# A gated MLP on linear attention: 1088 output columns cut into 364, 362 and 362 instead of 424, 332 and 332, with other starting addresses and a new order

## The chip, the cores and the metric

The kernel runs on one core of a Trainium2 chip. The metric is the device time of one execution in microseconds (us). A core has a matrix engine (TensorE, PE), three engines for element-wise work (VectorE or DVE, ScalarE or ACT, GpSimd or POOL), and SyncE (SP), which issues the DMAs here. Each engine runs its own instructions in the order in which they were written; engines wait for each other by semaphores.

## What is computed

```python
def _attn_ref(q, k, v, S1, S2):                     # 4 batches, 4 heads, 1088 positions, d = 32
    def phi(x):                                     # 8 x 8 = 64 features
        a = np.einsum('rd,bhsd->bhsr', S1, x)
        b = np.einsum('rd,bhsd->bhsr', S2, x)
        return np.einsum('bhsi,bhsj->bhsij', a, b).reshape(*x.shape[:-1], r * r)
    q_p, k_p = (phi(q), phi(k))
    kv = np.einsum('bhsf,bhsd->bhfd', k_p, v)
    z = np.sum(k_p, axis=2)
    num = np.einsum('bhsf,bhfd->bhsd', q_p, kv)
    den = np.einsum('bhsf,bhf->bhs', q_p, z)[..., None] + 1e-06
    return num / den

def _moe_ref(x, w_in, w_spatial, b_spatial, w_out): # x: 4 x 1088 x 128
    h = np.maximum(x @ w_in, 0.0)                   # 1024 wide
    u, v = (h[..., :512], h[..., 512:])
    v_n = (v - mean(v)) / np.sqrt(var(v) + 1e-06)
    v_s = np.einsum('ts,bsd->btd', w_spatial, v_n) + b_spatial[None, :, None]
    return (u * v_s) @ w_out                        # w_out: 512 x 128
```

## The kernel before

**Precision.** Every large product is made of two-part operands: a value is rounded to a "high" part and its remainder is the "low" part. `mm3` (L424) is then three matmuls: high by high (L425), high by low (L426), low by high (L427). `split` (L502) makes the parts: ACT casts the high one (L504), DVE subtracts to get the low one (L435), on POOL in some cases (L438).

**Tiling.** The 1088 output positions (the columns of a matmul's streamed operand) are cut into three chunks `CH`; the 512 gated features into four blocks d of 128; the 1088 input positions into nine row blocks kt (eight of 128 and one of 64). For each batch b, block d and chunk c (48 in all) `main` (L829) issues
- `hidden`: three matmuls of one `mm3` into the PSUM bank `pu` and a relu on ACT into a tile u (L935),
- `spatial`: 26 matmuls into a bank `sp`: nine L943 (vh by the high weights), eight L945 (vl by the high weights), eight L952 (vh by the low weights) and one L954 for the last row block, which has the bias in two extra rows,
- `gate`: DVE multiplies sp by u (L979) and the product is split into gh and gl,
- `out_mm`: three matmuls of one `mm3` into the bank `po`, which sums over d; after the last d, ACT or DVE copies it out (L917, L919) and SP stores it (L922).

v is the stationary operand (tiles vh, vl), the spatial weights are streamed (tile wT, high and low halves, with the bias rows in its last row block). Batch 0 goes through chunk 0 for all four d at once, first a high pass over kt (its four accumulators are in two sp and two po banks), then a low pass, because v's row blocks come one after another from the layer norm (L799 to L824, split by L889, L892 and L898, L901). The other (b, d, c) follow one by one. The attention of a batch runs beside the main part of the batch before it; batch 0's runs ahead (`attention0`).

**Loads.** Weights come in pieces through the staging tiles `pl` (L432), ACT casts the high part (L551), DVE or POOL subtracts the low part (L554). w_in and w_out are 64-bit floats and are decoded by integer arithmetic (L487 to L500). The bias is loaded once (b32), split, and each half is copied to a row of wT by DMAs on SP (L568), one for each piece of `BIAS`.

**Homes in memory.** Most tiles rotate through as many buffers as `SB_BUFS` says; an instruction that writes a new tile waits for the last reader of the old one in its buffer. Before, chunk 0 (424 columns) of batches 0 and 3 had homes of its own (`big`): u and the copied output in the kp tiles, and the two parts of the gate in the two buffers of the xh or xl tiles. All other gates use three u and three g buffers. Modulo 256 bytes, the stationary tiles vh, wih0, woh began at 96 and vl, wil0, wol at 224; chunk 0 of wT at 32 and chunks 1 and 2 at 240; g at 32 or 240.

**What sets the order.** All instructions are first collected by the class `Order` (L117) with their costs and readers, and are then put into one order for each engine by a list scheduler: due times come backwards from `T_MAIN`, `PACE` and the costs (`c_mm` from the table `C_MM` and so on), and the table `LEADS` moves groups or single instructions ahead or back by nanoseconds. Into gaps that the planner expects on PE in the first 50 us it puts small filling matmuls (L452).

## Time and profile before

| | us |
|---|---|
| median of 3 runs | 330.75 (330.46 to 331.38) |
| profiled execution | 331.01 |
| its span | 329.2 |
| main loop of batch 0 begins (first L943) | 31.84 |
| last matmul begins | 325.78 |

A row of the timeline is: start, duration, engine, line, operation, output<-inputs, shapes, count, and in brackets idle time of that engine just before and who ended it. Matmuls are pipelined: their durations overlap, and what one costs is the distance to the start of the next. A row of the windows view is: stretch, its length, then busy time and (count) of PE, PE's weight loads, DVE, ACT and POOL, the granted clock of PE, the share of the DMA engines and GB/s. SPq is SP's queue of DMA issues. Names are the program's, with buffer numbers left out.

### The profile page before, as it was taken

The page shows a single profiled execution, that of the slowest core. Times are in us where ns is not written, and L with a number is a line of the kernel's source. Part 1 is how long each engine was busy: PE and PEld are TensorE (multiplying, and loading weights), DVE is VectorE, ACT ScalarE, POOL GpSimd, SP SyncE. Part 2 cuts the span into 40 slices and gives each one's busy share as a digit, 9 for nine tenths or more (in the row PEclk, how much of TensorE's full clock was granted, in tenths as well). Part 3 has the DMA queues.
Part 4 walks back from the last instruction along what each step waited for, and adds up shares of the span by engine and source line. Part 5 has one row for each costly group of instructions (what it writes and reads, how often), then busy time and mean ns, then how long its engine had stood idle before and what let it go on. Part 6 is the DMA issues. An engine that isn't in the chain of part 4 may idle for free.

```text
span 329.2 us, 6032 instructions
## 1 busy us (share of the span) xinstructions
PE 323.0 (98%) x2308; PEld 311.2 (95%) x2308; DVE 200.3 (61%) x449; ACT 158.0 (48%) x365; POOL 59.4 (18%) x69
## 2 busy tenths in 40 slices
...
PEclk9999999999999999999999999999999999999999
...
GB/s 218 304 94 51 122 136 277 153 131 161 60 47 44 20 127 147 148 2 24 47 96 1 77 111 60 2 0 0 3 0 2 0 47 23 0 2 1 0 2 68
DMA packets 18365, 23.10 MB, mean 70 GB/s; under 512 B 3104, under 2 KB 18080, under 8 KB 18336
## 3 DMA queue, kind: packets, MB, share of 16 engines
...
q14 instruction: 11, 0.09, 0.1%
...
## 4 chain that ended last, share of the span: by engine, by line
PE 76%; DVE 9%; ACT 5%; DMA 5%; SPq 2%; issue 1%; DVEq 0%; ACTq 0%
PE sp L943 18%; PE sp L945 16%; PE sp L952 16%; PE sd L425 3%; PE sd L426 3%; PE sd L427 3%; PE po L426 2%; DMA pl<-in_wT 2%; PE pu L425 2%; SPq L432 2%; DVE wT L554 2%; PE pu L427 2%; PE pu L426 2%; PE po L427 2%; PE po L425 2%; PE sd L638 2%
## 5 line engine op out<-in xcount | busy, mean ns | idle before, releaser
L943 PE MATMUL sp<-wT,vh 128*128 128x332 f32 (+1 forms) x414 | 134.4, 325 | 0.0
L945 PE MATMUL sp<-wT,vl 128*128 128x332 f32 (+1 forms) x368 | 119.1, 324 | 0.0
L952 PE MATMUL sp<-wT,vh 128*128 128x332 f32 (+1 forms) x368 | 116.9, 323 | 0.0
L943 PEld LDWEIGHTS sp<-wT,vh 128*128 128x128 f32 x414 | 77.9, 188 | 1.3
L945 PEld LDWEIGHTS sp<-wT,vl 128*128 128x128 f32 x368 | 69.2, 188 | 0.6
L952 PEld LDWEIGHTS sp<-wT,vh 128*128 128x128 f32 x368 | 69.1, 188 | 0.2
L979 DVE TENSOR_TENSOR u<-sp,u 128x332 f32<-128x332 f32 (+1 forms) x40 | 20.5, 514 | 38.3 <-PE sp L954 26.9
L435 DVE TENSOR_TENSOR g<-u,g 128x332 fp32r<-128x332 f32 (+1 forms) x38 | 21.7, 570 | 25.7 <-PE po L426 18.9
L504 ACT CAST g<-u 128x332 fp32r<-128x332 f32 (+1 forms) x38 | 17.9, 485 | 40.2 <-DVE u L979 25.8
L935 ACT ACTIVATE u<-pu 128x332 f32<-128x332 f32 (+1 forms) x40 | 18.5, 463 | 36.1 <-PE pu L427 35.1
L801 DVE BATCH_NORM_STATS2 st<-vt 128x6 f32<-128x512 f32 x36 | 24.2, 688 | 5.1 <-ACT vt L799 4.9
L779 DVE RECIPROCAL c<-c 128x384 f32<-128x384 f32 (+1 forms) x9 | 21.8, 2418 | 9.2 <-ACT c L777 9.2
L799 ACT ACTIVATE vt<-sd 128x512 f32<-128x512 f32 x36 | 21.4, 601 | 10.9 <-PE sd L427 10.3
L748 POOL TENSOR_TENSOR pl<-pl,pl 128x384 f32<-128x384 f32 (+1 forms) x18 | 19.0, 1059 | 33.6 <-DMA pl<-abT 33.4
L861 ACT CAST vh<-vt 128x384 fp32r<-128x384 f32 x36 | 17.4, 510 | 14.4 <-DVE vt L821 8.4
L438 POOL TENSOR_TENSOR r<-pl,r 128x384 fp32r<-128x384 f32 (+1 forms) x18 | 17.5, 982 | 37.1 <-ACT r L504 37.0
L863 DVE TENSOR_TENSOR vl<-vt,vh 128x384 fp32r<-128x384 f32 (+1 forms) x36 | 20.2, 578 | 2.8 <-ACT vh L861 2.7
L821 DVE TENSOR_SCALAR vt<-vt,mv,sm 128x512 f32<-128x512 f32 x32 | 17.4, 579 | 0.0
L438 POOL TENSOR_TENSOR r<-c,r 128x384 fp32r<-128x384 f32 (+1 forms) x9 | 9.7, 1082 | 40.0 <-ACT r L504 40.0
L425 PE MATMUL pu<-x,wih 128*128 128x332 f32 (+1 forms) x48 | 16.0, 334 | 0.8 <-ACT kp L935 0.8
L426 PE MATMUL pu<-x,wih 128*128 128x332 f32 (+1 forms) x48 | 15.7, 327 | 0.0
L427 PE MATMUL pu<-x,wil 128*128 128x332 f32 (+1 forms) x48 | 15.7, 327 | 0.0
(161 smaller groups left out, 522.2 us busy)
## 6 DMA issues: line engine op xcount, KB each, us to landing
...
```

The lines of the kernel that those rows point to most:

```text
L425: nc.tensor.matmul(o, ah, bh, start=start, stop=False)
L426: nc.tensor.matmul(o, ah, bl, start=False, stop=False)
L427: nc.tensor.matmul(o, al, bh, start=False, stop=stop)
L435: return lambda: nc.vector.tensor_tensor(out=o(), in0=a(), in1=bb(), op=ALU.subtract)
L438: return lambda: nc.gpsimd.tensor_tensor(out=o(), in0=a(), in1=bb(), op=ALU.subtract)
L779: op("DVE", 135 + 6.3 * n, lambda x32=x32, n=n: nc.vector.reciprocal(out=x32[:, :n], in_=x32[:, :n]), w=[x32])
L799: op("ACT", c_act(512, True), lambda pv=pv, t=t: nc.scalar.activation(vt[:, t], pv.ap, AF.Relu), r=[pv], w=[(vt, t)])
L801: op("DVE", 690, lambda stats=stats, t=t: nc.vector.bn_stats(out=stats.ap, in_=vt[:, t]), r=[(vt, t)], w=[stats])
L943: nc.tensor.matmul(sp[:, :cw], vh[:, kt], wTh[:, kt, cs], start=(kt == 0), stop=False)
L945: nc.tensor.matmul(sp[:, :cw], vl[:, kt], wTh[:, kt, cs], start=False, stop=False)
L952: nc.tensor.matmul(sp[:, :cw], vh[:, kt], wTl[:, kt, cs], start=False, stop=False)
L979: op("DVE", c_dve(cw), lambda: nc.vector.tensor_tensor(out=u.ap, in0=sp[:, :cw], in1=u.ap, op=ALU.mult), r=[sp], w=[u], lead=LEAD[1])
```

## The change

- The chunks are 364, 362 and 362 columns wide and begin at 0, 384 and 768 of a row block's 1152.
- wT, the g and the r buffers lie in one tile `moving` that is shifted by four elements, so that each of them begins at 176 modulo 256 bytes. The six stationary tiles follow each other, and all begin at 160. x now begins at 0 (32 before) and the second half of w_in, which is streamed too, at 64 (160 before).
- `big` is gone: every gate of every batch uses the three u and the three g buffers (r in the last block, as before), and the output copies use u (vt in the last batch).
- `pl` has seven buffers instead of six.
- The bias is cut into five pieces instead of three (364, 360 and 2, 360 and 2 columns), so ten instead of six DMAs copy it to wT.
- `C_MM` has the new sizes, and nearly all of `LEADS`'s 1,600 numbers are new. The order is new on every engine; fewer filling matmuls are put in.

```diff
-CH = [(0, 424), (424, 332), (756, 332)]
-AT = [0, 436, 820]
-PITCH, G_PITCH, G_AT = 1152, 448, {424: 0, 332: 52}
-BIAS = [(0, 8, 53), (8, 4, 83), (12, 4, 83)]
+CH = [(0, 364), (364, 362), (726, 362)]
+AHEAD, LINE = 4, 64
+AT = [0, 384, 768]
+PITCH = 1152
+BIAS = [(0, 4, 91), (4, 4, 90), (8, 2, 1), (10, 4, 90), (14, 2, 1)]
+BIAS_AT = [(0, 0), (1, 0), (1, 360), (2, 0), (2, 360)]
...
-    "pl": 6, "c": 3, "r": 4, "abT": 2, "kt": 3, "v": 3, "ka": 2, "kp": 3, "kvh": 1, "kvl": 1,
+    "pl": 7, "c": 3, "r": 4, "abT": 2, "kt": 3, "v": 3, "ka": 2, "kp": 3, "kvh": 1, "kvl": 1,
...
-LEADS = {'W0': 13650, 'W0.0': -12650, 'W0.2': -20000, 'W0.3': -8660, 'W0.4': -12950,
+LEADS = {'W0': 12110, 'W0.0': 1680, 'W0.1': 19860, 'W0.3': 18270, 'W0.4': -770, 'W0.5': -8890,
...
-C_MM = {424: 188.5, 332: 148.5}
+C_MM = {364: 162.0, 362: 161.0}
 def c_mm(n, k=1):
...
-    homes["ka", 0] = const.tile([P, 96], F32, name="ka0")
-    fixed["b32"], fixed["mask_sb"] = const.tile([P, 16], F32, name="b32"), const.tile([P, 6], F32, name="mask_sb")
-    weights("vh", "wih0", "woh")
-    homes["ka", 1] = const.tile([P, 96], F32, name="ka1")
-    weights("vl", "wil0", "wol")
+    fixed["mask_sb"] = const.tile([P, 6], F32, name="mask_sb")
+    weights("vh", "vl", "wih0", "wil0", "woh", "wol")
+    n_w, n_g, n_r = 2 * NS * PITCH, SB_BUFS["g"] * 384, SB_BUFS["r"] * 384
+    moving = const.tile([P, 2 * AHEAD + n_w + n_g + n_r], F32R, name="moving")[:, AHEAD:]
+    homes["wT"] = moving[:, :n_w]
+    homes |= {("g", i): moving[:, n_w + 384 * i:n_w + 384 * (i + 1)] for i in range(SB_BUFS["g"])}
+    homes |= {("r", i): moving[:, n_w + n_g + 384 * i:n_w + n_g + 384 * (i + 1)] for i in range(SB_BUFS["r"])}
...
-    homes["wT"] = const.tile([P, 2 * NS * PITCH], F32R, name="wT")
-    homes["g"] = const.tile([P, SB_BUFS["g"], G_PITCH], F32R, name="g")
...
-        if t.tag == "g":
-            at = G_AT[t.shape[1]]
-            return homes["g"][:, t.slot, at:at + t.shape[1]]
...
     def load_bias():
-        b32 = tl(None, "b32", [83, 16])
+        b32 = tl(None, "b32", [91, 16])
...
-        bh, bl = tl(None, "bh", [83, 16], F32R), tl(None, "bl", [83, 16], F32R)
+        bh, bl = tl(None, "bh", [91, 16], F32R), tl(None, "bl", [91, 16], F32R)
...
-        for c, (at, w, rows) in enumerate(BIAS):
+        for (at, w, rows), (c, c0) in zip(BIAS, BIAS_AT):
...
-                cs = slice(AT[c], AT[c] + w * rows)
+                cs = slice(AT[c] + c0, AT[c] + c0 + w * rows)
...
-                    r=[t], w=[(wTl, ("bias", c, n))], kb=2,
+                    r=[t], w=[(wTl, ("bias", c, c0, n))], kb=2,
...
     def load_sq():
...
-        def big(c):
-            return c == 0 and (wide or not b)
...
         def due(cost):
...
-                ob = tl("vt" if wide else "kp" if big(c) else "u", f"ob{b}{c}", [P, cw])
+                ob = tl("vt" if wide else "u", f"ob{b}{c}", [P, cw])
...
                 def copy(eng, at, n, key):
...
-            u = tl("kp" if big(c) else "u", f"u{b}{d}{c}", [P, cw])
+            u = tl("u", f"u{b}{d}{c}", [P, cw])
...
-                r += [(wTl, (kt, c))] + ([(wTl, ("bias", c, 0)), (wTl, ("bias", c, 1)), vx] if kt == NK else [])
+                r += [(wTl, (kt, c))] + ([*((wTl, ("bias", c, c0, n)) for x, c0 in BIAS_AT if x == c for n in range(2)), vx] if kt == NK else [])
             def f():
...
         def gate(d, c, sp, u):
...
-            if big(c):
-                g = tl(("xh", "xl")[d % 2], f"g{b}{d}{c}", [P, 2, G_PITCH], F32R)
-                parts = [(lambda: g[:, 0, :cw], (g, 0)), (lambda: g[:, 1, :cw], (g, 1))]
-            else:
-                tag = "r" if last(d) else "g"
-                gh, gl = tl(tag, f"gh{b}{d}{c}", [P, cw], F32R), tl(tag, f"gl{b}{d}{c}", [P, cw], F32R)
-                parts = [(lambda: gh.ap, gh), (lambda: gl.ap, gl)]
-            (hi, wh), (lo, wl) = parts
-            split(hi, lo, lambda: u.ap, cw, [u], [wh], [wl])
-            return hi, lo, [wh, wl]
+            tag = "r" if last(d) else "g"
+            gh, gl = tl(tag, f"gh{b}{d}{c}", [P, cw], F32R), tl(tag, f"gl{b}{d}{c}", [P, cw], F32R)
+            split(lambda: gh.ap, lambda: gl.ap, lambda: u.ap, cw, [u], [gh], [gl])
+            return lambda: gh.ap, lambda: gl.ap, [gh, gl]
...
-    bias = np.zeros((83, 16), moe_b_spatial.dtype)
-    for (c0, cw), (at, w, rows) in zip(CH, BIAS):
-        bias[:rows, at:at + w] = moe_b_spatial.reshape(-1)[c0:c0 + cw].reshape(rows, w)
+    bias = np.zeros((91, 16), moe_b_spatial.dtype)
+    for (at, w, rows), (c, c0) in zip(BIAS, BIAS_AT):
+        c0 += CH[c][0]
+        bias[:rows, at:at + w] = moe_b_spatial.reshape(-1)[c0:c0 + w * rows].reshape(rows, w)
...
```

Line numbers behind the table of sizes are 2 lower in the new kernel (L425 is L423, L554 is L552), and 6 lower in `main` (L943 is L937).

**SP, from the last weight pieces ahead of the bias to w_out.** Rows are line, operation, output<-source, shape. pl is a staging tile, bh and bl are the bias's halves. Before:

```order
L432 DMA pl_229<-in_wT 128x424
L432 DMA pl_77<-in_wT 128x424
L568 DMA wT<-bh 1x53x8
L568 DMA wT<-bh 1x83x4 x2
L568 DMA wT<-bl 1x53x8
L568 DMA wT<-bl 1x83x4 x2
L432 DMA pl_196<-in_wT 128x424
L432 DMA kt<-in_w_out 128x4x256
L432 DMA pl_187<-in_wT 128x424
```

Now:

```order
L430 DMA pl_246<-in_wT 128x364
L430 DMA pl_80<-in_wT 128x364
L566 DMA moving<-bh 1x91x4
L566 DMA moving<-bh 1x2x1 x2
L566 DMA moving<-bh 1x90x4 x2
L566 DMA moving<-bl 1x91x4
L566 DMA moving<-bl 1x2x1 x2
L430 DMA pl_224<-in_wT 128x364
L566 DMA moving<-bl 1x90x4 x2
L430 DMA kt<-in_w_out 128x4x256
L430 DMA pl_222<-in_wT 128x364
```

Ten bias DMAs instead of six stand ahead of the load of w_out (kt<-in_w_out). Further ahead, the cast of bh, for which the first of them waits, stood on ACT behind three casts of weights; now it stands ahead of them.

**DVE, around the low halves of v's row blocks 6 and 7 of batch 0** (the L892 x2 of before, L886 x2 now). Rows are line, operation, output<-inputs, shape; L554 and L552 make the low part of a piece of the weights, L821 and L819 normalise a block of v. Before:

```order
L812 SCALAR_TENSOR_TENSOR sm_507<-sm_517,sm_507 128x3
L554 TENSOR_TENSOR wT<-pl_187,wT 128x424
L812 SCALAR_TENSOR_TENSOR sm_537<-mv_474,sm_507 128x3
L554 TENSOR_TENSOR wT<-pl_77,wT 128x424
L821 TENSOR_SCALAR vt_164<-vt_164,mv_474,sm_507 128x512
L554 TENSOR_TENSOR wT<-pl_196,wT 128x424
L821 TENSOR_SCALAR vt_164<-vt_164,mv_474,sm_507 128x512
L892 TENSOR_TENSOR vl<-vt_164,vh 128x512 x2
L554 TENSOR_TENSOR wT<-pl_227,wT 64x424
L901 TENSOR_TENSOR vh<-vt_164,vh 64x512
```

Now:

```order
L810 SCALAR_TENSOR_TENSOR sm_512<-sm_520,sm_512 128x3
L552 TENSOR_TENSOR moving<-pl_222,moving 64x364
L810 SCALAR_TENSOR_TENSOR sm_543<-mv_481,sm_512 128x3
L886 TENSOR_TENSOR vl<-vt_98,vh 128x512
L819 TENSOR_SCALAR vt_161<-vt_161,mv_481,sm_512 128x512 x2
L886 TENSOR_TENSOR vl<-vt_161,vh 128x512 x2
L552 TENSOR_TENSOR moving<-pl_191,moving 128x364
L488 TENSOR_SCALAR v<-v 128x512
L552 TENSOR_TENSOR moving<-pl_224,moving 128x364
L552 TENSOR_TENSOR moving<-pl_207,moving 128x362
L895 TENSOR_TENSOR vh<-vt_161,vh 64x512
```

Ahead of the two low halves stood three low parts of chunk 0's weights in these rows, and one stands there now; the others moved behind them, among decoding steps of w_out (L488).

**PE, the first output product of chunk 1 in batch 0** (po_146<-g before, po_121<-moving now, where moving is the streamed tile that also holds g). Before:

```order
L945 MATMUL sp_301<-wT,vl 128x332
L952 MATMUL sp_301<-wT,vh 128x332
L425 MATMUL po_261<-x,woh 128x424
L426 MATMUL po_261<-x,woh 128x424
L427 MATMUL po_261<-x,wol 128x424
L425 MATMUL po_146<-g,woh 128x332
L426 MATMUL po_146<-g,woh 128x332
L427 MATMUL po_146<-g,wol 128x332
L943 MATMUL sp_301<-wT,vh 128x332
L945 MATMUL sp_301<-wT,vl 128x332
```

Now:

```order
L636 MATMUL sd_123<-v,kp_144 64x66 x12
L636 MATMUL sd_123<-v,kp_157 64x66 x12
L937 MATMUL sp_262<-moving,vh 128x362
L948 MATMUL sp_262<-moving,v_83 128x362
L937 MATMUL sp_302<-moving,vh 128x362
L939 MATMUL sp_302<-moving,vl 128x362
L946 MATMUL sp_302<-moving,vh 128x362
L423 MATMUL po_121<-moving,woh 128x362
L424 MATMUL po_121<-moving,woh 128x362
L425 MATMUL po_121<-moving,wol 128x362
```

Before, this product came right behind the last output product of chunk 0, and its gate stood on DVE behind that chunk's; now it stands 87 rows further on, behind 36 small attention products (L636, twelve a row) and more of the spatial stream.

2 lines of the change are left out of this document (1 added, 1 removed).

## The prediction

> **What bounds the kernel now.** I read the page's busy shares and chain first, then busy time by stretch, then the timeline, where the starts of successive matmuls give what one of them costs (their durations overlap). The durations come from one profiled execution of 331.01 us, of which 329.2 us is the span; the median of the runs shown is 330.75, 0.26 lower.
>
> ```profile
> PE 323.0 (98%) x2308; PEld 311.2 (95%) x2308; DVE 200.3 (61%) x449; ACT 158.0 (48%) x365; POOL 59.4 (18%) x69
> PEclk9999999999999999999999999999999999999999
> 31.80:43.40 11.60, 11.60 (x60) 11.16 (x59) 11.46 (x28) 9.86 (x23) 2.33 (x2) 1.00 0.45 130
> 200.00:300.00 100.00, 100.00 (x607) 98.36 (x607) 47.11 (x103) 36.12 (x82) 5.38 (x7) 1.00 0.02 8
> ```
>
> TensorE is busy 98% of the span at the full granted clock, and in the stretch from 200 to 300 us nothing else comes near. The time is therefore the sum of matmul gaps, plus a few stalls, plus the start and the end. Only in the first 50 us is another engine as full: from 31.8 to 43.4 DVE is busy 11.46 of 11.60 us. So four things can change: the gap of a matmul, the stalls, the prologue, the tail.
>
> **Size of a matmul.** Each row block is now streamed in 364, 362 and 362 columns instead of 424, 332 and 332. The columns (1088) and the matmuls are the same. There are 16 pairs of batch and block, with 26 spatial, 3 hidden and 3 output matmuls for each chunk, so 32 x 16 = 512 triples of matmuls.
>
> ```profile
> 222.70 0.31 PE L943 MATMUL sp<-wT,vh 128*128 128x332 f32 x1
> ...
> 226.66 0.39 PE L425 MATMUL sd<-wih,x 128*128 128x512 f32 x1
> 233.33 0.35 PE L943 MATMUL sp<-wT,vh 128*128 128x424 f32 x1
> ...
> 234.09 0.35 PE L945 MATMUL sp<-wT,vl 128*128 128x424 f32 x1
> ...
> 237.08 0.32 PE L943 MATMUL sp<-wT,vh 128*128 128x332 f32 x1
> ```
>
> From 222.70 to 226.66 stand 27 matmuls of 332 columns: 146.7 ns each. From 234.09 to 237.08 stand 16 of 424: 186.9 ns. The four just before, after the change of size, took (234.09 - 233.33) / 4 = 190 ns: a stream needs a few matmuls to settle. The line through 146.7 and 186.9 gives 160.7 at 364 and 159.8 at 362, so a triple costs 480.3 before and after: **0 by this line**. Short runs of the same sizes can be read too:
>
> ```profile
> 150.35 0.31 PE L425 MATMUL pu<-x,wih 128*128 128x332 f32 x1
> ...
> 150.81 0.32 PE L425 MATMUL po<-g,woh 128*128 128x332 f32 x1
> 24.64 0.36 PE L425 MATMUL pu<-x,wih 128*128 128x424 f32 x1
> ...
> 25.22 0.39 PE L425 MATMUL sd<-wih,x 128*128 128x512 f32 x1
> 47.10 0.34 PE L425 MATMUL sd<-r,sqh 128*128 128x384 f32 x1
> ...
> 47.62 1.12 PE L952 MATMUL sp<-wT,vh 128*128 128x424 f32 x5
> ```
>
> Three of 332 take 0.46 us (153 each), three of 424 take 0.58 (193), three of 384 take 0.52 (173). The line from 153 to 193 would give 176 at 384; the measured 173 lies below it. By the line from 332 to 384 a triple would cost 165.3 + 164.5 + 164.5 = 494.3 instead of 193 + 2 x 153 = 499: 5 ns less, or 2.6 us in 512 triples. I keep both ends, 0 and -2.6, and take 2 ns a triple, nearer to the settled row because most of the stream is long runs: **-1.0 us**. No other engine is as full there, so all of it lies on the path.
>
> The Trainium skill (TensorE: Matmul & The Clock Gate, Back-to-back issue gap) gives the gap of an isolated warm matmul as columns / 2.4 plus 2.5 ns. By it a triple costs 460.8 ns under either cut, so the cut alone would change nothing; the trace's 146.7 at 332 columns is 5.9 ns above that rule's 140.8 and its 186.9 at 424 is 7.7 above 179.2, so the trace does not bear the fixed 2.5 out.
>
> The new starting addresses (176 modulo 256 bytes for what is streamed, 160 for the weights) I cost at nothing: the stream of before settles alike on weights at 96 and at 224, vh and vl alternating in the rows above. That it doesn't settle on the new ones is a rival below.
>
> **Breaks.** Counted in the two orders, the spatial stream is cut by other matmuls into 125 pieces before and 111 now, and 775 against 715 matmuls stand among the first nine of a piece. At 190 - 186.9, about 3 to 5 ns each, 60 fewer of them are **-0.25 us**.
>
> **Stalls.** Two output products waited on the split of their gate:
>
> ```profile
> 62.85 0.31 PE L425 MATMUL po<-g,woh 128*128 128x332 f32 x1
> 63.52 0.42 PE L426 MATMUL po<-g,woh 128*128 128x332 f32 x1 [0.35 <-DVE g L435]
> 63.77 0.31 PE L427 MATMUL po<-g,wol 128*128 128x332 f32 x1
> 107.06 0.31 PE L425 MATMUL po<-g,woh 128*128 128x332 f32 x1
> 107.92 0.41 PE L426 MATMUL po<-g,woh 128*128 128x332 f32 x1 [0.56 <-DVE g L435]
> 108.17 0.31 PE L427 MATMUL po<-g,wol 128*128 128x332 f32 x1
> ```
>
> Against 0.15 a matmul, the first lost 0.52 + 0.10, the second 0.71 + 0.10: 1.4 us together. The new order puts the first product of chunk 1 87 rows further down, past 36 small products, and the others also further behind their gates, so these waits go. What is late next is batch 0's supply from DVE:
>
> ```profile
> 37.72 0.59 DVE L554 TENSOR_TENSOR wT<-pl,wT 128x424 fp32r<-128x424 f32 x1
> 38.23 0.54 DVE L821 TENSOR_SCALAR vt<-vt,mv,sm 128x512 f32<-128x512 f32 x1
> ...
> 39.20 1.24 DVE L821 TENSOR_SCALAR vt<-vt,mv,sm 128x512 f32<-128x512 f32 x1
> 40.36 1.28 DVE L892 TENSOR_TENSOR vl<-vt,vh 128x512 fp32r<-128x512 f32 x2
> 39.13 1.03 POOL L438 TENSOR_TENSOR r<-c,r 128x384 fp32r<-128x384 f32 x1 [5.27 <-ACT r L504]
> ```
>
> PE now runs through chunk 0's high pass at 364/424 of its pace (about 0.167 instead of 0.195 a matmul) and asks for row block 6's low half at the 48th matmul, 31.84 + 47 x 0.167 = 39.7; before it had it at 40.96 (the pair of 40.36 ends at 41.57, 0.60 each). The new DVE order takes two weight rows from ahead of it (2 x 0.51) and shortens the two that remain (2 x 0.06): 39.8. The L821 of 39.20 took 1.24 beside POOL's L438, against 0.46 for the one of 38.23; if the two part, 39.1. So the margin is between -0.1 and 0.6, and the same at row block 8 and at the last low weight rows of chunk 0. For these, and for other products now tight behind their gates, I allow 0.8 in all. Net **-0.6 us**; bounds -1.4 and +1.2.
>
> **Prologue.** Ten bias transfers instead of six stand on SP ahead of w_out:
>
> ```profile
> 8.23 0.31 SPq L432 DMA_DIRECT2D b<-in_bsp  x1
> 15.99 2.04 SPq L568 DMA_DIRECT2D wT<-bh  x3
> 18.13 1.83 SPq L568 DMA_DIRECT2D wT<-bl  x3
> 20.06 0.53 SPq L432 DMA_DIRECT2D pl<-in_wT  x1
> 20.69 0.69 SPq L432 DMA_DIRECT2D kt<-in_w_out  x1
> 15.76 0.21 ACT L504 CAST bh<-b 83x16 fp32r<-83x16 f32 x1
> 25.20 0.67 ACT L487 ACTIVATE v<-kt 128x512 f32<-128x512 f32 x1 [0.46 <-DMA kt<-in_w_out]
> 26.45 0.52 ACT L935 ACTIVATE kp<-pu 128x424 f32<-128x424 f32 x1
> 27.02 0.46 PE L425 MATMUL pu<-x,wih 128*128 128x424 f32 x1 [0.61 <-ACT kp L935]
> 31.84 0.36 PE L943 MATMUL po<-wT,vh 128*128 128x424 f32 x1
> ```
>
> ACT waits 0.46 for w_out; behind it in ACT's row stands the L935 that empties the bank for the hidden product, for which PE waits 0.61, and from there PE runs without a gap into the main loop at 31.84. So a later w_out moves the main loop one for one. The bias cast now comes ahead of two weight casts and one of 512 columns instead of behind them, some 1.4 us earlier at about 0.45 each. Six long transfers at 2.04 / 3 to 1.83 / 3 and four of two elements at between 0.31 (the issue of b) and 0.61 make 5.1 to 6.4 instead of 3.97: w_out is issued 0 to 1.3 us later. The small matrices S1 and S2 (in_sks) are now loaded second on SP instead of first, and one filler stands ahead of PE's first projection (some 0.25); that is hidden by ACT's 0.46, and gone with it. I take **+0.6 us** (0 to 1.3).
>
> **Tail.**
>
> ```profile
> 324.13 0.50 DVE L435 TENSOR_TENSOR g<-u,g 128x332 fp32r<-128x332 f32 x1
> 325.78 0.32 PE L427 MATMUL po<-r,wol 128*128 128x332 f32 x1
> 326.13 0.44 ACT L917 COPY vt<-po 128x332 f32<-128x332 f32 x1 [0.87 <-PE po L427]
> ```
>
> Five output triples again follow the last gate. One split now reuses a g tile two triples after its last reader; its chain of 0.94 (two of 0.50, overlapping) just fits 2 x 0.48. The copies grow by 0.02. **+0.1 us**.
>
> **Sum:** -1.0 - 0.25 - 0.6 + 0.6 + 0.1 = -1.15 on 331.01 = 329.86 by the profiled execution; against the median 330.75, **329.6 us**.
>
> **Rivals.**
> 1. **No change**: the size term is 0 by the settled line and the removed stalls come back whole at other gates (0 - 0.25 + 0 + 0.6 + 0.1): 331.2; with half of the stalls gone 330.3; about 330.75. For it: every product still has its gate's split ahead of it on DVE. Against: the longer distances. The rule of the Trainium skill named above also gives 0 for the size term.
> 2. **Slower, the stream doesn't settle** at the new addresses, in all spatial runs. About half of the 1,536 matmuls, some 700, now stand at the settled 147 and 187; each would pay 3.1 (190 - 186.9) to 6.3 (153 - 146.7): 2.2 to 4.5 us. 333.0. It decides from about half of them on.
> 3. **Slower, three small homes**: chunk 0's gates of batch 0 had wide homes; now four gates share three u and three g tiles, a gate's low half waits for an earlier output product, and DVE, which runs in order, holds the weight rows behind it. Three such waits at the price of those above (0.62 to 0.81) are +2.2 us: 331.8, or 332 where w_out is late as well. It decides once DVE is over 0.3 us later than in my walk.
> 4. **Much faster**: the size term at its low end and no new waits: 329.6 - 1.6 - 0.8 = 327.2.
>
> **Chances.** Forecast (328.6 to 330.6) 0.45, rival 1 0.20, rival 2 0.09, rival 3 0.13, rival 4 0.13. The range reaches from rival 4 to past rival 3, 327.0 to 332.7, leaving out half of rival 4, most of rival 2 and the far ends. A measurement of this kernel tells about 0.3% (1.0 us) from no change. Faster than 329.76: rival 4, 0.6 of the forecast and a little of rival 1, 0.42. Slower than 331.74: rival 2, most of rival 3 and a little of rival 1, 0.23. Within: 0.35.
>
> **What would show it.** Gaps in a long run of 364 near 160 (right), 165 or more (rival 2). ACT's wait for w_out at 0.5 to 1.7 us, and the first spatial matmul at 32.4. No wait of PE on L433 at the first product of chunk 1; waits between 38 and 46 us below 0.6. PE's last matmul about 3 us before the span's end. Wrong would make it a wait that appears in batches 1 and 2, which I went through only by distances.

## The result, and the profile after

The changed kernel takes **339.27 us** (median of 4 runs, 338.85 to 340.18) against 330.62 us for the kernel before (4 runs beside it): a ratio of **1.0261, 95% interval 1.0234 to 1.0288**. It is slower, and outside of the range that was given. The profiled execution took 339.48 us, with a span of 337.7 against 329.2.

From the page of the changed kernel, the busy times and TensorE's granted clock by slices:

```profile
PE 327.2 (97%) x2304; PEld 313.9 (93%) x2304; DVE 204.7 (61%) x449; ACT 159.1 (47%) x365; POOL 61.6 (18%) x69
PEclk9999999999999999999999999999999999999999
```

Busy time by stretch (PE, PEld, DVE, ACT and POOL with their counts, then the clock), first two stretches of the kernel before, then three of the changed kernel:

```profile
31.84:60.00 28.16, 28.16 (x156) 27.56 (x155) 22.97 (x50) 19.62 (x47) 9.38 (x9) 1.00 0.66 191
90.00:130.00 40.00, 39.44 (x270) 37.05 (x270) 32.39 (x74) 23.43 (x59) 12.78 (x13) 1.00 0.36 72
```

```profile
33.69:60.00 26.31, 25.37 (x150) 24.25 (x149) 25.69 (x53) 19.19 (x44) 7.97 (x7) 1.00 0.61 180
90.00:130.00 40.00, 37.91 (x218) 35.76 (x217) 34.13 (x75) 25.38 (x60) 11.30 (x12) 1.00 0.30 64
200.00:300.00 100.00, 100.00 (x685) 97.96 (x684) 50.60 (x110) 40.08 (x92) 10.83 (x12) 1.00 0.10 22
```

In this execution the granted clock is whole throughout, so a lower clock explains nothing of it. (The other three runs have a mean granted clock of 0.993 to 0.995, and no trace says where it fell; their times, 338.85 to 340.18, lie on both sides of this one.) TensorE, idle 0.56 us between 90 and 130 before, is idle 2.09 there now. From the start of the main loop to 60 us it was never idle before, with DVE busy 22.97 of 28.16 us; now it is idle 0.94, with DVE busy 25.69 of 26.31. From 200 to 300 us it is full as before. So the loss lies in the start, in the first 130 us, and in what a matmul costs.

TensorE's waits in the changed kernel (total, times, longest, all in us; a row of the prologue is left out):

```profile
PE pu L423 <- ACT u L929: 3.0, 4, 2.2
PE sp L937 <- DVE u L973: 1.7, 2, 1.1
...
PE po L937 <- DVE vh L895: 0.7, 1, 0.7
```

I measured where the span grew by following every matmul's start to the next one's, and counting as a wait what lies over 60 ns above the usual gap of its size. The differences add up to the 8.4 us by which the span grew (329.24 to 337.67), within the rounding:

| | before | after | difference |
|---|---|---|---|
| start of the first spatial product, us | 31.84 | 33.69 | +1.9 |
| waits of TensorE from there on, us (times) | 2.48 (14) | 7.33 (36) | +4.9 |
| spatial gaps without waits, us | 202.31 | 203.66 | +1.35 |
| hidden and output products | | | +0.1 |
| from the last matmul's start to the end, us | 3.46 | 3.79 | +0.3 |

(Spatial: 424 columns at a mean of 190.23 ns and 332 at 149.04 before, 364 at 166.22 and 362 at 162.46 after.)

**The start.** SP, then ACT, then TensorE in the changed kernel's timeline (start, duration, and in brackets the idle time just before with what ended it):

```profile
14.94 4.01 SPq L566 DMA_DIRECT2D moving<-bh  x5
19.06 2.11 SPq L566 DMA_DIRECT2D moving<-bl  x3
21.27 0.35 SPq L430 DMA_DIRECT2D pl<-in_wT  x1
21.67 1.74 SPq L566 DMA_DIRECT2D moving<-bl  x2
23.51 0.50 SPq L430 DMA_DIRECT2D kt<-in_w_out  x1
27.30 0.66 ACT L485 ACTIVATE v<-kt 128x512 f32<-128x512 f32 x1 [2.08 <-DMA kt<-in_w_out]
29.05 0.44 PE L423 MATMUL pu<-x,wih 128*128 128x364 f32 x1 [2.25 <-ACT u L929]
33.69 0.33 PE L937 MATMUL po<-moving,vh 128*128 128x364 f32 x1
```

The ten bias transfers hold SP for 4.01 + 2.11 + 1.74 = 7.86 us, and w_out is issued at 23.51 instead of 20.69. The ACT row that decodes w_out waits 2.08 instead of 0.46 us, the copy of a hidden product queued behind it holds TensorE for 2.25, and the main loop starts 1.85 us later.

**A matmul.** Part of a late stream of the changed kernel, where nothing waits:

```profile
226.99 0.33 PE L939 MATMUL sp<-moving,vl 128*128 128x364 f32 x1
...
228.66 0.33 PE L946 MATMUL sp<-moving,vh 128*128 128x364 f32 x1
...
230.15 0.32 PE L946 MATMUL sp<-moving,vh 128*128 128x362 f32 x1
...
231.75 0.32 PE L937 MATMUL sp<-moving,vh 128*128 128x362 f32 x1
```

From 226.99 to 228.66 lie ten gaps of 364 columns, 167 ns each; from 230.15 to 231.75 ten of 362, 160 ns each. Two columns more cost 7 ns, not the 1 ns of the prediction's line.

**The waits.** Two of the largest are for a gate (L973) that comes late on DVE. The rows of DVE ahead of the second, then of POOL beside them, then TensorE's:

```profile
119.40 1.22 DVE L857 TENSOR_TENSOR vl<-vt,vh 128x384 fp32r<-128x384 f32 x3
120.63 1.01 DVE L864 TENSOR_TENSOR vh<-vt,vh 64x128 fp32r<-64x128 f32 x1
123.53 0.29 DVE L864 TENSOR_TENSOR vh<-vt,vh 64x128 fp32r<-64x128 f32 x1
123.84 0.54 DVE L973 TENSOR_TENSOR u<-sp,u 128x364 f32<-128x364 f32 x1
119.60 1.90 POOL L746 TENSOR_TENSOR pl<-pl,pl 128x384 f32<-128x384 f32 x1 [5.87 <-DMA pl<-abT]
124.44 0.44 PE L937 MATMUL sp<-moving,vh 128*128 128x362 f32 x1 [1.15 <-DVE u L973]
```

The L864 of 120.63 takes 1.01 us; the same operation at 123.53 takes 0.29. The long one lies beside a POOL row that ran from 119.60 to 121.50, itself 1.90 us long where the mean of its form is 1.10. I marked every DVE row that took over 0.2 us more than its form does (the shortest fifth of its form as the measure): in the changed kernel 18 rows, 11.2 us in all, in the kernel before 14 rows, 7.3 us; every one of them overlaps a POOL row. This sum is called the **stretch** below. How long they take follows POOL. The weight rows of 362 and 364 columns (L552, 0.53 us alone) that began 0.23, 0.36 and 0.56 us into a POOL row took 1.35, 1.29 and 1.35, and each ended 0.39 us after that POOL row did: such a row does not finish before POOL's row has ended. Not every row of DVE is held like this. Of the 50 that began within a POOL row of the changed kernel (0.1 us or more before its end), 16 ended before it did, among them seven of the eight gates (L973, which read one operand from a PSUM bank).

### The profile page after: what moved, and what is told of

Same layout as the page of the kernel before. It is cut to its first block, busy times and chain, and to the rows that moved or that the text cites. A ratio compares the mean times of both kernels' runs of the same rounds, so it can differ in the third digit from the quotient of the medians.

```text
span 337.7 us, 6016 instructions
## 1 busy us (share of the span) xinstructions
PE 327.2 (97%) x2304; PEld 313.9 (93%) x2304; DVE 204.7 (61%) x449; ACT 159.1 (47%) x365; POOL 61.6 (18%) x69
## 3 DMA queue, kind: packets, MB, share of 16 engines
HBM read 13.78 MB, written 2.23 MB: 47 GB/s over the span
## 4 chain that ended last, share of the span: by engine, by line
PE 72%; DVE 13%; ACT 6%; DMA 5%; issue 2%; SPq 1%; ACTq 0%
PE sp L937 17%; PE sp L946 15%; PE sp L939 15%; PE sd L425 3%; PE sd L423 3%; PE sd L424 2%; PE pu L423 2%; PE po L424 2%; DVE moving L552 2%; PE pu L424 2%; PE pu L425 2%; PE po L425 2%; PE sd L636 2%; PE po L423 2%; PE sp L948 2%
## 5 line engine op out<-in xcount | busy, mean ns | idle before, releaser
L937 PE MATMUL sp<-moving,vh 128*128 128x362 f32 (+1 forms) x414 | 135.9, 328 | 1.7 <-DVE u L973 1.7
L939 PE MATMUL sp<-moving,vl 128*128 128x362 f32 (+1 forms) x368 | 119.9, 326 | 0.0
L946 PE MATMUL sp<-moving,vh 128*128 128x362 f32 (+1 forms) x368 | 118.1, 326 | 0.0
L937 PEld LDWEIGHTS sp<-moving,vh 128*128 128x128 f32 x414 | 78.1, 189 | 3.1 <-DVE u L973 2.3
L939 PEld LDWEIGHTS sp<-moving,vl 128*128 128x128 f32 x368 | 69.4, 189 | 0.3
L946 PEld LDWEIGHTS sp<-moving,vh 128*128 128x128 f32 x368 | 69.0, 188 | 0.0
L973 DVE TENSOR_TENSOR u<-sp,u 128x362 f32<-128x362 f32 (+1 forms) x46 | 24.5, 532 | 61.3 <-PE sp L948 39.2
L502 ACT CAST moving<-u 128x362 fp32r<-128x362 f32 (+1 forms) x48 | 23.3, 495 | 45.9 <-DVE u L973 25.4
L433 DVE TENSOR_TENSOR moving<-u,moving 128x362 fp32r<-128x362 f32 (+1 forms) x48 | 28.0, 584 | 21.5 <-PE po L424 14.4
L929 ACT ACTIVATE u<-pu 128x362 f32<-128x362 f32 (+1 forms) x48 | 22.7, 473 | 36.5 <-PE pu L425 28.9
L436 POOL TENSOR_TENSOR moving<-pl,moving 128x384 fp32r<-128x384 f32 (+1 forms) x18 | 18.3, 1022 | 65.3 <-ACT moving L502 65.3
L797 ACT ACTIVATE vt<-sd 128x512 f32<-128x512 f32 x36 | 21.5, 600 | 15.6 <-PE sd L425 14.9
L855 ACT CAST vh<-vt 128x384 fp32r<-128x384 f32 x36 | 16.9, 510 | 11.4 <-DVE vt L819 7.8
L423 PE MATMUL pu<-x,wih 128*128 128x362 f32 (+1 forms) x48 | 16.3, 340 | 3.0 <-ACT u L929 3.0
L819 DVE TENSOR_SCALAR vt<-vt,mv,sm 128x512 f32<-128x512 f32 x32 | 16.3, 558 | 0.0
L425 PE MATMUL po<-moving,wol 128*128 128x362 f32 (+1 forms) x48 | 15.8, 329 | 0.0
```

Of the source, the lines that this page charges most:

```text
L423: nc.tensor.matmul(o, ah, bh, start=start, stop=False)
L425: nc.tensor.matmul(o, al, bh, start=False, stop=stop)
L433: return lambda: nc.vector.tensor_tensor(out=o(), in0=a(), in1=bb(), op=ALU.subtract)
L436: return lambda: nc.gpsimd.tensor_tensor(out=o(), in0=a(), in1=bb(), op=ALU.subtract)
L502: op("ACT", c_act(n), lambda: nc.scalar.copy(out=hi(), in_=x()), r=r, w=wh)
L929: op("ACT", c_act(cw, True), lambda: nc.scalar.activation(u.ap, pu[:, :cw], AF.Relu), r=[pu], w=[u], lead=LEAD[0])
```

## The experiments

In the table, "start" is that of the first spatial product, "waits" are TensorE's from there on, and the stretch is as above; these three come from one profiled execution each. The ratio is against runs of the kernel before on the same chip; these took 331.38 to 331.57 beside the experiments and 330.62 beside the changed kernel, so kernels of different rows are compared by their ratios.

| kernel | median, us | ratio (95%) | start | waits | stretch |
|---|---|---|---|---|---|
| before | 330.62 | | 31.84 | 2.48 | 7.3 |
| after | 339.27 | 1.0261 (1.0234 to 1.0288) | 33.69 | 7.33 | 11.2 |
| bias_late | 336.63 | 1.0156 (1.0135 to 1.0177) | 31.53 | 6.83 | 10.8 |
| old_with_addresses | 334.30 | 1.0084 (1.0062 to 1.0106) | 32.23 | 3.05 | 8.3 |
| new_with_old_table | 342.32 | 1.0338 (1.0313 to 1.0363) | 35.53 | 6.91 | 14.1 |
| gates_moved | 339.20 | 1.0236 (1.0199 to 1.0272) | 31.56 | 10.81 | 11.8 |
| homes_back | 340.71 | 1.0287 (1.0251 to 1.0323) | 31.26 | 9.52 | 11.4 |
| sizes_alone | 339.66 | 1.0245 (1.0224 to 1.0266) | 32.40 | 7.80 | 8.8 |
| old_moved | 332.21 | 1.0019 (1.0008 to 1.0031) | 32.73 | 4.34 | 9.2 |
| before_new_table | 337.08 | 1.0167 (1.0139 to 1.0195) | 31.73 | 7.61 | 10.8 |
| phase_208 | 336.73 | 1.0160 (1.0119 to 1.0200) | 31.63 | 7.15 | 11.1 |
| pool_short_new | 338.72 | 1.0210 (1.0183 to 1.0238) | 36.45 | 2.52 | 2.5 |
| pool_short_old | 335.11 | 1.0080 (1.0036 to 1.0124) | 37.30 | 2.19 | 3.3 |
| short_new | 334.61 | 1.0087 (1.0059 to 1.0114) | 32.93 | 3.60 | 2.0 |
| short_old | 330.65 | 0.9977 (0.9950 to 1.0003) | 31.73 | 2.01 | 1.5 |

One execution's starts and waits are not exact: phase_208 has the order of bias_late, and the changed kernel has it too but for the bias transfers, and the three show waits of 6.83 to 7.33. Three of the profiled executions had the granted clock at a half for a while: new_with_old_table from 30.2 to 33.6 us, just ahead of its late start, gates_moved from 47.7 to 51.1, and pool_short_new from 8.8 to 15.6. In new_with_old_table a gap of 364 columns was 301 to 305 ns in that time.

### gaps: what a matmul costs, by size and address

A kernel that does nothing of the reference's but stream: 69 settings of 39 matmuls each, in the order of the kernel's (vh on the high half, vl on the high half, vh on the low half), with size and start addresses set.

```diff
+    for i, (n, m, w0, w1) in enumerate(CONF):
...
+            nc.tensor.matmul(o[:, :n], vh, hi, start=(r == 0), stop=False)
+            nc.tensor.matmul(o[:, :n], vl, hi, start=False, stop=False)
+            nc.tensor.matmul(o[:, :n], vh, lo, start=False, stop=(r == REP - 1))
```

> Leaves out the whole computation: 39 matmuls in a row at each of 69 pairs of column count and starting address, nothing beside them, to measure the settled gap of a triple (vh by high, vl by high, vh by low). Theory A (steps): in the traces the settled gaps are 146.67 at 332 columns, 160.00 at 362, 166.67 at 364 and 186.67 at 424, all multiples of 6.67 ns; so the gap rises in steps of 6.67 ns every 16 columns, with a step between 362 and 364 at the new address 176, and the place of the step moves with the streamed operand's address, so that 364 falls to 160.0 at some of them. Theory B (line): the gap rises by 0.42 to 0.44 ns a column from 146.7 at 332 to 186.9 at 424, 364 alone stands at 160.5 at every address, and the 166.7 of 364 in the changed kernel comes from what is around it there.

Four settings in its timeline, all with the streamed operand at 176 and the weights at 160 modulo 256 bytes:

```profile
33.03 0.31 PE L60 MATMUL b<-big,wt 128*128 128x332 f32 x1
...
34.79 0.31 PE L60 MATMUL b<-big,wt 128*128 128x332 f32 x1
94.50 0.32 PE L60 MATMUL b<-big,wt 128*128 128x362 f32 x1
...
96.42 0.32 PE L60 MATMUL b<-big,wt 128*128 128x362 f32 x1
100.93 0.33 PE L60 MATMUL b<-big,wt 128*128 128x364 f32 x1
...
102.93 0.33 PE L60 MATMUL b<-big,wt 128*128 128x364 f32 x1
169.81 0.35 PE L59 MATMUL b<-big,wt 128*128 128x424 f32 x1
...
171.68 0.35 PE L60 MATMUL b<-big,wt 128*128 128x424 f32 x1
```

Twelve gaps of 332 columns take 1.76 us, of 362 1.92, of 364 2.00, and ten of 424 take 1.87: over the settled half of each setting, 146.7, 160.0, 166.7 and 186.7 ns. The other sizes show why a line fails: 332 columns stand at 146.7, 336 and 340 at 153.3, 348 to 356 and 362 at 160, 364, 366, 372 and 376 at 166.7, 380 at 173.3, 416 and 424 at 186.7. So the mean gap goes largely in **steps of 6.67 ns**: 14 of the 25 sizes up to 424 settle within 0.4 ns of a multiple of it, and the others between two. (It is the mean that does: at 332, 362 and 424 columns every gap is alike, while at 416 they are 182 and 191 by turns.) It does not even rise all the way: 330 columns (150.1), 360 (164.4) and 420 (189.7) cost more than 332, 362 and 424. These three are the last sizes of their steps, and 364 is on the next one. A triple costs 480.0 ns in the old cut and 486.7 in the new one.

The addresses matter too. With weights at 160, 332 columns take 146.7 ns from 144 or 176, 150.0 from 240, and 153.3 from 0, 32, 64, 112 or 208; 362 take 160.0 from 176 and 163.3 to 166.7 from all seven others tried. So 176 is a good address for 362 columns; 364 take 165.3 to 168.9 from eleven of the twelve addresses tried, and 162.2 from 208. With weights at 96 and 224 in turn, the old kernel's pair, 332 columns take 146.7 from 240 and 424 take 186.7 from 32, where with weights at 160 the same two take 150.0 and 193.3. So the pair of addresses counts, with the size. That they count modulo 256 bytes was taken as given and not tried.

### bias_late: the queue ahead of w_out

```diff
     order = k.schedule()
+    late = [o for o in order if not isinstance(o, Fill) and o.eng == "SP" and any(isinstance(x[0][1], tuple) and x[0][1][0] == "bias" for x in o.rw)]
...
+    order = [o for o in order if o not in late]
+    at = next(i for i, o in enumerate(order) if not isinstance(o, Fill) and o.name == "wo_raw:1") + 1
+    order[at:at] = late
```

> The changed kernel with one edit: the ten bias transfers stand behind the load of w_out on SP, everything else in the same order. Theory A (queue): the ten transfers took 7.9 us on SP and are what made w_out late; without them ahead of it w_out lands at or before 25.1, ACT's wait for it goes from 2.1 to below 0.5, the first spatial matmul comes at 31.5 to 32.0 instead of 33.7, and the time falls by 1.5 to 2.0 us, to 337.3 to 337.8. Theory B (saturated): ACT and DVE are full in this stage, the wait only moves, the main loop begins at 33 or later and the time stays above 338.5.

336.63 us, a ratio of 1.0156 against the changed kernel's 1.0261. That is a larger gain than theory A named (337.3 to 337.8): its start comes 2.2 us earlier, and its waits are 0.5 less. In its timeline:

```profile
20.38 0.39 SPq L430 DMA_DIRECT2D kt<-in_w_out  x1
20.82 4.01 SPq L566 DMA_DIRECT2D moving<-bh  x5
24.87 3.86 SPq L566 DMA_DIRECT2D moving<-bl  x5
24.88 0.66 ACT L485 ACTIVATE v<-kt 128x512 f32<-128x512 f32 x1
28.24 0.43 PE L423 MATMUL pu<-x,wih 128*128 128x364 f32 x1 [0.17 <-ACT u L929]
31.53 0.33 PE L937 MATMUL po<-moving,vh 128*128 128x364 f32 x1
```

w_out is issued ahead of the bias, ACT does not wait for it, and the loop starts at 31.53 instead of 33.69. The bias transfers still cost 7.87 us, where nothing waits for them. That the queue cost the start is shown. The waits in the loop hardly change (7.33 to 6.83), so they have another cause; the next kernels look for it from here.

### old_with_addresses, phase_208: addresses in the kernel

The kernel before with nothing but its homes placed otherwise: weights at 160, what is streamed at 176 (332 columns) and 224 (424).

```diff
-    weights("vh", "wih0", "woh")
...
+    weights("vh", "vl", "wih0", "wil0", "woh", "wol")
...
+    moving = const.tile([P, AHEAD + n_w + n_g + n_r], F32R, name="moving")[:, AHEAD:]
+    homes["wT"] = moving[:, :n_w]
...
```

> The kernel before with its own chunks, homes and order, and only other addresses: all weights at 160, the 332-column chunks of the streamed operand at 176, the 424-column chunk at 224 (modulo 256 bytes). Theory A (order and waits make the 8.6 us): settled gaps stay at 146.7 and 186.7 or move by one step of 6.67 ns, no new waits, 330.6 within 1.0 if no step moves, and 333.5 if the 332s (two thirds of the matmuls) move up by one step. Theory B (the addresses make the 8.6 us): 337 to 340.

334.30 us, between what theory A named (330.6 to 333.5) and theory B (337 to 340), and nearer to A: the addresses alone do not make the loss. The loop's waits are 3.05. The mean spatial gap rises from 190.23 to 193.15 ns at 424 columns (1.2 us over 414 of them) and from 149.04 to 151.03 at 332 (1.65 over 829). A stretch of its timeline shows how:

```profile
222.23 0.31 PE L953 MATMUL sp<-moving,vh 128*128 128x332 f32 x1
...
223.55 0.31 PE L953 MATMUL sp<-moving,vh 128*128 128x332 f32 x1
225.31 0.32 PE L953 MATMUL sp<-moving,vh 128*128 128x332 f32 x1
...
228.99 0.32 PE L953 MATMUL sp<-moving,vh 128*128 128x332 f32 x1
```

From 222.23 to 223.55 lie nine gaps, 147 ns each; from 225.31 to 228.99 24, 153 ns each. Same size, same addresses, and yet a stream can stay on the upper step for as long as it runs; why is open. So the new addresses do not serve the old cut: the "slower, the stream doesn't settle" of my rivals, for the cut that they weren't chosen for.

In bias_late, 364 columns moved to the one address that was better alone:

```diff
-AT = [0, 384, 768]
+AT = [8, 384, 768]
```

> bias_late (336.63 us) with one number changed: the 364 columns of the weights start 8 columns later in their home, at 208 modulo 256 bytes instead of 176. In the run of gaps alone, 364 columns settled at 162.2 ns there and at 166.7 at 176. Theory A (the address sets the gap in the kernel too): the mean start to start of the 364-column products falls from 166.2 to 162 to 163.5 ns, 1.1 to 1.8 us over 415 of them, and the time to 334.6 to 335.8. Theory B (within the kernel's order, with weights that alternate, the address does not matter at this size): the mean stays above 165 and the time between 336.0 and 337.3.

336.73 us, a ratio of 1.0160 against 1.0156: no gain that can be measured. The mean gap at 364 columns falls from 166.69 to 165.01 ns, 0.7 us in all, which is just within theory B's bounds (above 165): of the gaps between two such matmuls 45% still stand at 166 to 168, and the settled 162.2 of the run alone is not reached in the kernel's shorter, mixed runs.

### new_with_old_table, before_new_table: the table of lead times

```diff
-LEADS = {'W0': 12110, 'W0.0': 1680, 'W0.1': 19860, 'W0.3': 18270,
...
+LEADS = {'W0': 13650, 'W0.0': -12650, 'W0.2': -20000, 'W0.3': -8660,
...
```

> The changed kernel with the kernel before's table LEADS, carried over name by name; chunks, homes, addresses and ten bias transfers stay as changed. Theory A (the new table makes most of the 4.9 us of new waits): PE's waits of over 60 ns sum to 2.5 to 4 us instead of 7.3, and the time is 335 to 337. Theory B (the missing wide homes and the sizes make the waits, and the new table was fitted to them): the waits sum to 7 us or more and the time is 339 to 343.

342.32 us, waits 6.91, and a later start (35.53, with the clock at a half just ahead of it). Going back to the old table does not take the waits away, so the new table alone was not their cause. The other way round, the kernel before with the changed kernel's table:

> The kernel before with nothing changed but the table of lead times, which is the changed kernel's. Theory A (a table fits only the kernel whose durations it was made with): TensorE's waits in the main loop 6 to 10 us instead of 2.5, time 334 to 340. Theory B (the waits of the changed kernel come of its cut, homes or queue, and either table serves either kernel): waits at most 4 us, time 330 to 332.5.

337.08 us, waits 7.61. Two of the rows of its list:

```profile
PE po L426 <- DVE g L435: 0.9, 1, 0.9
PE sp L943 <- DVE u L979: 0.7, 2, 0.4
```

The cut, homes, addresses and transfers of before, all left as they were, wait as long as the changed kernel as soon as the order is another one. Of the four pairs of kernel and table, three wait 6.9 to 7.6 us, and only the old kernel with its old table waits 2.5.

### homes_back, sizes_alone: the homes and the cut

bias_late with the wide homes of chunk 0's gates restored:

```diff
+        def big(c):
+            return c == 0 and (wide or not b)
...
-            u = tl("u", f"u{b}{d}{c}", [P, cw])
+            u = tl("kp" if big(c) else "u", f"u{b}{d}{c}", [P, cw])
```

> The run bias_late with the wide homes of chunk 0 of batches 0 and 3 back (u and the copied output in kp, the gate's parts in xh or xl); the scheduler makes a new order with the new table. Theory A (without these homes gates and output copies share three tiles, and that makes the waits): the waits of PE on g and on u in batch 0 (0.8 and 0.5 us) go, the sum of the waits of over 60 ns falls from 6.8 to 4.5 or less, and the time to 334 to 335.5. Theory B (the table's order makes them): the sum stays at 5.5 to 8 and the time within 1.2 us of 336.6 or above.

340.71 us, waits 9.52: slower, not faster. The scheduler makes a new order for these homes, so this run alone doesn't clear the small ones; the next one has the wide homes too. It has only the new cut and addresses in the kernel before, with its table, its homes, its six staging tiles and six bias transfers, and again an order of its own:

```diff
-CH = [(0, 424), (424, 332), (756, 332)]
-AT = [0, 436, 820]
+CH = [(0, 364), (364, 362), (726, 362)]
...
+AT = [0, 384, 768]
...
```

> The kernel before's table, homes, six staging tiles and six bias transfers (each of 364 columns, two of them not used in chunks 1 and 2), with the new chunks and the new addresses. Theory A (cut and addresses cost only their gaps): a triple's settled gap is 486.7 instead of 480.0 ns, less what more even runs win, so +1.4 us as in the changed kernel; PE's waits stay at 2 to 3.5 us, w_out is no later than before, and the time is 331.5 to 333. Theory B (the table fits only its own chunks, so any other cut brings waits): the waits are 5 us or more and the time is 335 to 339.

339.66 us, waits 7.80, just above the upper end that theory B named. The cut and the addresses, under the old table and with the wide homes, bring waits as large as the whole change does, so the small homes are not needed for them. Its longest wait:

```profile
84.33 2.55 DVE L777 RECIPROCAL c<-c 128x384 f32<-128x384 f32 x1 [3.16 <-ACT c L775]
87.33 0.43 PE L940 MATMUL sp<-moving,vh 128*128 128x362 f32 x1 [1.45 <-DVE u L976]
```

The gate L976 stands on DVE right behind this reciprocal, which takes the usual time (the mean of its line in the changed kernel is 2.42). That is a wait of the order alone.

### gates_moved, old_moved: rows moved by hand

In bias_late, seven DVE rows that stood ahead of the awaited rows of 44, 115 and 124 us, put behind them. Some of the moved rows then read a rotating tile after its next writer, so part of the values of batches 0 and 1 are other ones.

```diff
...
+    behind(("wTl:8", "wo_x:2"), "vh00:10")
+    behind(("st122:1",), "u022:2")
+    behind(("vl13:2", "vh12:4", "vh11:4", "vh13:4"), "u100:2")
```

> The run bias_late with seven DVE instructions put behind the one that PE waits for, at three places: two rows (a low weight part, a decoding step) behind L895 of batch 0, one L799 behind the gate L973 that PE waited for at 112.1 to 112.9 in bias_late, four parts of batch 1's v (L857, L864) behind the gate that it waited for at 120.8 to 122.3. Nothing else moves. Theory A (DVE works its row in order, and what stands ahead of a gate is the wait): the three waits of 0.94, 0.82 and 1.42 us go to about 0.1, 0.2 and 0.1, the time falls by 2.3 to 2.9 us against bias_late, to 333.7 to 334.3. Theory B (the waits only move to the next instruction that DVE is late for): the sum of PE's waits stays above 6 us and the time falls by less than 1.

339.20 us, waits 10.81 instead of 6.83: the two waits for gates are gone, and others, for rows that now stand further down, take their place, the largest for two weight rows. About 1.6 of the 10.81 are no waits but 12 gaps beside the half clock of 47.7 to 51.1 us. The first row of its list:

```profile
PE po L946 <- DVE moving L552: 1.9, 2, 1.1
```

The same by hand in the kernel before, for the stalls that my prediction wanted gone: the bias behind w_out, and three output products put behind later work.

```diff
...
+    for name, after in (("po01:1", "sp011:8"), ("po02:1", "pu022:1"), ("po02:3", "pv120:1")):
+        move(name, after, "PE")
```

> The kernel before with its six bias transfers behind w_out, and the three output products that waited for their gates (62.85, 94.2, 107.06) put two, one and three operations later on PE. Theory A (the waits are of place): w_out lands before ACT asks for it, the main loop begins at 31.3 to 31.6 instead of 31.83, the waits of 0.62, 0.2 and 0.81 go, and the time falls by 1.5 to 2.1 us, to a ratio of 0.994 to 0.9955. Theory B (the time is set elsewhere): within 0.5 us of before.

332.21 us, ratio 1.0019 (1.0008 to 1.0031). The two waits at the output products go, and others come (a gate for 1.1 us among them): 4.34 in all instead of 2.48. The profiled execution was the slowest of ten (333.68), and its start, 32.73, is late although w_out no longer waits for the bias: the second half of w_in is decoded from 15.01 there, and from 13.78 in the kernel before. By the time of all runs, what I counted as a gain of the stalls is none when it is tried by itself.

### pool_short_new, pool_short_old, short_new, short_old: DVE beside POOL

In the main loop of the changed kernel and of bias_late, each of TensorE's waits for DVE of over 0.4 us has a stretched row not far ahead of what it waits for. So POOL's rows were shortened to 8 columns, in the same order; the rest of what they compute is left out. In pool_short_new that is all of its subtractions and products; the other three keep the low halves of batch 1's queries whole.

```diff
     def sub_pool(o, a, bb):
-        return lambda: nc.gpsimd.tensor_tensor(out=o(), in0=a(), in1=bb(), op=ALU.subtract)
+        return lambda: nc.gpsimd.tensor_tensor(out=o()[:, :8], in0=a()[:, :8], in1=bb()[:, :8], op=ALU.subtract)
...
+                if n_pool == 3:
...
+                    nc.gpsimd.memset(wTl[:, :NS - 1, AT[2]:AT[2] + CH[2][1]].bitcast(F32), 0.0)
```

> The changed kernel with its ten bias transfers behind w_out (bias_late, 336.63 us), and GpSimd's subtractions and products done on their first 8 columns alone: the low halves of the weights of chunk 2, of the queries and of their products, and the products themselves, are left out but for these columns (the weights' and the queries' low halves are filled with zeros in the prologue). The order of every engine stays. In bias_late every VectorE row that took over 0.2 us more than its form does lay beside a GpSimd row, 10.8 us in all. Theory A: these stretched rows make TensorE's waits. Their sum falls below 2.5 us, TensorE's waits in the main loop from 6.8 to at most 3.5 us, and the time to 332 to 334. Theory B: the waits come of the order, whose rows are due late for their readers with or without the stretch: waits above 6 us, time 335.5 to 337.5.

> The same in the kernel before (330.6 us): GpSimd's subtractions and products on 8 columns, but for the queries of batch 1, whose low halves stay whole; the rest of them is left out. It is the control for pool_short_new. VectorE's stretch there is 7.3 us, TensorE's waits in the main loop 2.5. Theory A (the table of before leaves room for its own stretched rows): waits 1 to 2.5 us, time 329.0 to 331.0, so that pool_short_new gains at least 2 us more than this one. Theory B (short GpSimd rows help any kernel alike): the same gain as in pool_short_new within 1 us.

The loop did what theory A said: in pool_short_new the stretch in the main loop goes to nothing and the waits from 6.83 to 2.52 us; in the control they go from 2.48 to 2.19. From the first spatial product to the start of the last matmul, pool_short_new needs 295.6 us where bias_late needs 299.9, and the control 293.5 where the kernel before needs 293.95. The times did not follow, 338.72 and 335.11 us: the filling with zeros, on POOL in the prologue, stretched a DVE row there by 2.5 and 1.7 us, and the loop of the profiled execution began about 5 us later in both. (The rest of these 5 us was not looked into, but for pool_short_new's half clock; and three of pool_short_old's ten runs took 331.2 to 331.3, the others 333.5 to 336.4, so its start is not always late.) So the same was tried with nothing to fill, chunk 2 reading the high half of its weights twice:

```diff
+            x = wTh if c == 2 else wTl
...
-                nc.tensor.matmul(sp[:, :cw], vh[:, kt], wTl[:, kt, cs], start=False, stop=False)
+                nc.tensor.matmul(sp[:, :cw], vh[:, kt], x[:, kt, cs], start=False, stop=False)
```

> bias_late (336.63 us; first spatial product at 31.5 us, TensorE's waits in the main loop 6.8 us) with GpSimd's subtractions and products on 8 columns, and nothing filled: the spatial products of chunk 2 read the high half of the weights in place of the low half, the low halves of the other queries than batch 1's and of the products, and the products themselves, are left as they are in their buffers but for 8 columns. So the low half of chunk 2's weights and most of GpSimd's work are left out. Theory A (VectorE rows stretched beside GpSimd rows make the waits): first spatial product at 31 to 32.5, waits at most 3.5 us, time 331.5 to 333.5. Theory B (the waits come of the order, and pool_short_new lost them because its loop began 5 us later): waits above 5.5 us, time 335 to 337.5.

> The same cut of GpSimd's work in the kernel before (330.6 us, waits 2.5 us). Theory A: waits 1.5 to 2.5 us, time 329 to 331: its gain is at most 1.5 us, against 3 to 5 us in short_new. Theory B (short GpSimd rows help any order alike): the same gain as in short_new within 1 us.

short_new takes 334.61 us, 2.0 less than bias_late (2.3 by the ratios); theory A had named 331.5 to 333.5, theory B 335 to 337.5, and it lies between them. The waits fall to 3.60, near A's 3.5. The profiled execution's start, 32.93, is 1.4 later than bias_late's, because the second half of w_in landed later there (its decode begins at 15.32 instead of 13.88); up to 13.8 us the two timelines are alike. short_old takes 330.65, 0.2% less than the kernel before and not told apart from it, with waits of 2.01. The rows ahead of the gate that came late at 123.84 in the changed kernel, in bias_late and then in short_new:

```profile
116.62 2.71 POOL L746 TENSOR_TENSOR pl<-pl,pl 128x384 f32<-128x384 f32 x1 [5.07 <-DMA pl<-abT]
118.46 1.02 DVE L864 TENSOR_TENSOR vh<-vt,vh 64x128 fp32r<-64x128 f32 x1
122.27 0.43 PE L937 MATMUL sp<-moving,vh 128*128 128x362 f32 x1 [1.15 <-DVE u L973]
```

```profile
117.21 0.25 POOL L747 TENSOR_TENSOR pl<-pl,pl 128x8 f32<-128x8 f32 x1 [6.05 <-DMA pl<-abT]
117.41 0.29 DVE L865 TENSOR_TENSOR vh<-vt,vh 64x128 fp32r<-64x128 f32 x1
119.91 0.54 DVE L975 TENSOR_TENSOR u<-sp,u 128x364 f32<-128x364 f32 x1
```

The row takes 0.29 us instead of 1.02, and no wait of TensorE's for a gate is left in short_new's list. So of the 4.35 us that bias_late waits more than the kernel before, short POOL rows take 3.2 - 0.5 = 2.8. Nearly a half of the 1.6 left is a wait with a stretched row ahead of it still, beside one of batch 1's rows that stayed whole (POOL, DVE, TensorE in short_new):

```profile
40.79 1.18 POOL L436 TENSOR_TENSOR moving<-c,moving 128x384 fp32r<-128x384 f32 x1 [5.73 <-ACT moving L502]
41.01 1.35 DVE L553 TENSOR_TENSOR moving<-pl,moving 128x364 fp32r<-128x364 f32 x1
44.37 0.44 PE L938 MATMUL po<-moving,vh 128*128 128x364 f32 x1 [0.54 <-DVE vh L896]
```

TensorE's matmul before this one began at 43.50, so that 0.7 us are lost. In pool_short_new this POOL row takes 0.38, the weight row behind it 0.54, and the wait is gone; there, with no stretched row in the loop, the waits are down to the kernel before's (2.52 against 2.48), though its loop began 4.9 us later than bias_late's, which may have helped. So the stretch accounts for 2.8 us of the 4.35 at least, and perhaps for nearly all. Short POOL rows also hand on their own results earlier; that this helped was not tried apart, though TensorE's waits for POOL in bias_late are too small to be listed.

None of these kernels beats the kernel before.

## Why the prediction was wrong

**Size of a matmul (forecast -1.0, with breaks -1.25; measured +1.45).** The step that failed is "the line through 146.7 and 186.9 gives 160.7 at 364 and 159.8 at 362". The two points were right, and both are the ends of steps; 362 costs the 160.0 that the line gave, and 364 costs 166.7, on the next step. Settled, the new cut costs 6.7 ns a triple more, 3.4 us in 512; that only 1.45 came is because the old cut was further from settling on average (190.23 against 186.7, 149.04 against 146.7) than the new one (166.22 against 166.7, 162.46 against 160.0). The other end of that term, -2.6, came from a row of 384 columns, and had the wrong sign as well.

**New addresses (costed at nothing).** Right for 362 columns, for which 176 with 160 is the only one of the eight addresses tried that settles at 160.0. That "the stream of before settles alike on weights at 96 and at 224" was no evidence, since it had other streamed addresses beside them: the pair counts. The second rival's price, 2.2 to 4.5 us, was paid in old_with_addresses, with 2.8. Seen from the forecast's sign (gaps of 364 at 165 or more), the second rival seems to have come true; gaps shows that it did not: 364 settles, at 166.7.

**Prologue (forecast +0.6, 0 to 1.3; measured +1.9).** The mechanism was right, link by link, and was undone by bias_late. Mis-sized was the price of a transfer: 0.31 to 0.61 for those of two elements and 0.61 to 0.68 for the long ones. The last two long ones take 1.74 / 2 = 0.87, and the three ahead of the weight piece 2.11, of which one long one of about 0.87 leaves about 0.62 for each short one: 7.86 us in all, against the 5.1 to 6.4 taken. The price of the long ones came from pieces of 53 and 83 rows (0.58 to 0.71), and these have 90 or 91 (0.78 to 0.93). The earlier cast of the bias gave back 1.05 (14.94 instead of 15.99).

**Stalls (forecast -0.6, at most +1.2; measured +4.9).** The two waits that I wanted gone did go. What came in their place I looked for between 38 and 46 us, and found a margin of -0.1 to 0.6; a wait of 0.92 came there at 44, behind a weight row of DVE (41.75) that took 1.35 beside POOL. The two largest others came behind gates at 115 and 124, the second in batch 1: that is the wait "in batches 1 and 2, which I went through only by distances". The row that gave the mechanism away stood in my own prediction: an L821 of 1.24 us beside POOL's L438 against 0.46. I took it for one place, to be put right if the two part, and not for a cost of every order, which moves from row to row as the order moves. The Trainium skill (SBUF — State Buffer, Who interferes with whom) has the rule that I did not weigh: a VectorE instruction with two inputs in SBUF, or in one of its faster two-port modes, and a GpSimd instruction that reads SBUF exclude each other, and the one that comes second blocks until the first has ended. The trace agrees: the long L552 rows end 0.39 us after the POOL row, whenever they began. The scheduler of both kernels allows for it (L290 and L291 of the kernel before let an operation marked `sh` end behind the POOL operation that it meets), but at the times that it plans; where the rows meet on the chip is another matter. So the step that failed is to carry the old order's small waits over to a new order by distances alone: of the four pairs of kernel and table, only the old one waits 2.5 us.

**Rivals.** The slower rival of three small homes named waits of gates, the right kind, but not the right cause: the waits come with the wide homes too (sizes_alone 7.80, homes_back 9.52). No rival said that any other order would wait, which is what before_new_table shows.

**Tail (forecast +0.1; measured +0.3).** Not looked into.

**Slips in the working.** Some numbers do not follow from the rows beside them: the ten transfers come to 4.9 to 6.5 us by their own prices, not 5.1 to 6.4; 494.3 against 499 is 4.7 ns a triple and 2.4 us, not 5 and 2.6; the first rival with half of the stalls gone is 330.5 by the 1.4 us of its rows, not 330.3; and the pair of low halves that begins at 40.36 ends at 41.64. None of them moves the forecast by over 0.2 us.

What stays open: why every order but the old one waits about 7 us or more. The stretch is shown as a cause in bias_late alone, which has the changed kernel's order. sizes_alone waits 7.80 with a stretch of 8.8, hardly more than old_with_addresses with 8.3 and 3.05: the sum of the stretch does not tell the waits, and sizes_alone's longest has no stretched row ahead of it. How either table was made is not on record; that the old one fits its own kernel's real durations is how I read the four pairs, and is not shown. The prologue's start varies by over 1 us between single profiles with the landing of w_in, which blurs any reading of it below that.
